# Sending a block's second half of output rows from the next block, and the last one behind all branches

## The chip, the cores and the metric

One core of one Trainium2 chip. The metric is the time of one execution on the device in microseconds (us), the median of several runs. Engine names are those of the profile: PE (TensorE matmul), DVE (VectorE), ACT (ScalarE), POOL (GpSimd), SP (SyncE); a q behind a name marks the engine's sequencer, which handles waits, branches and semaphore counts.

## The reference

Three stages on 4608 tokens of 512 numbers:

```python
attn = softmax(q @ mean8(k).T / 8); x = attn @ mean8(v)     # 8 batches, 8 heads
x = softplus(x @ w_in) @ w_out                              # 512 -> 2048 -> 512
do = x @ w_skip > 0                                         # tokens that compute
e = argmax(x @ w_gate); gate = softmax(x @ w_gate)[e]       # one of 8 experts
out = x;  out[do] = x + gate * (relu(x @ w1[e]) @ w2[e])    # 512 -> 1024 -> 512
```

The change lies in the last stage, the experts.

## The kernel before

The first two stages run over 9 groups of 512 tokens (up to 907 us of the span) and leave every token's row, with its gate weight, in a table in HBM; tokens that don't compute are written to `out` at once (L197). A table of token numbers, sorted by expert, says which rows belong together.

The expert stage (from 907 us) works on blocks of 256 rows of one expert: two halves of 128 rows. `superblock(i)` (L863) is one block. Blocks 0 to 9 are each in an If of their own (L870); from block 10 on the Ifs are nested (L964 to L967), each block inside that of the block before, so that the first block that doesn't exist skips all the rest with one jump. Twenty blocks run with these inputs. What a block does, by engine:

- PE multiplies the block's transposed rows with the first weight matrix (L898, 96 matmuls of 256 columns), then the result, half by half, with the second (L922 to L924, 24 matmuls of 512 columns for each half). The second half is in an If of its own in the nested blocks (L918), and is left out where a block has at most 128 rows: 38 halves are computed in 20 blocks.
- ACT and DVE take the results out of PSUM (L902, L903), split the next weights into two parts (`split1` L401, `split2` L409), and DVE makes the output rows of half j, `ys[j]` (L926).
- POOL issues the indirect DMAs, one after the other from one queue: the next block's weights (`fetch` L394), rows for later blocks (`gather` L354), token numbers for later blocks (`load_ids` L347), and the sends of `ys[0]` and `ys[1]` to `out` (L928), at the rows that `ids[i % 5]` names. Row numbers that don't exist are above the bounds and are dropped.

The order on each engine's queue is that of the code here (L932 switches the scheduler's reordering off). The framework adds the waits: the two sends write the same tensor, so the second waits until the first has landed; at an If whose body is skipped, each engine raises its own semaphore by what the body would have raised, and POOL does so for the semaphores of its DMAs, after it has waited for the DMAs that came before. At the end of the program SP waits for all semaphores, every engine drains, and POOL collects them all.

In a block, POOL's queue thus ends with

```python
nc.gpsimd.indirect_dma_start(
    out=out, out_offset=bass.IndirectOffsetOnAxis(ap=ids[i % 5][:, j:j + 1], axis=0),
    in_=ys[j], in_offset=None, bounds_check=NTOK - 1, oob_is_err=False)
```

for j = 0 and j = 1, and the next block begins with `fetch("raw1", w1, i + 1)` (L874).

Of the kernel before, what the change touches and what calls it, by code (L numbers as in the profile page):

```python
# [12 lines left out]
I32 = mybir.dt.int32  # L13
# [7 lines left out]
P = 128  # L21
# [9 lines left out]
BIG = float(1 << 20)  # L31
# [5 lines left out]
def tile_kernel(ctx, tc, qT, kT, vT, wbits, w9, w1, w2, out):  # L37
    nc = tc.nc
    NTOK = out.shape[0]
# [52 lines left out]
    ids = [const.tile([P, 2], I32, name=f"ids{i}") for i in range(5)]  # L92
# [251 lines left out]
    def at(i):  # L344
        return (lists[1], i) if i < NS1 else (lists[2], i - NS1)

    def load_ids(i):  # L347
        li, s = at(i)
        nc.gpsimd.indirect_dma_start(  # L349
            out=ids[i % 5], out_offset=None, in_=tab,  # L350
            in_offset=bass.IndirectOffsetOnAxis(ap=li["tidx"][:, s:s + 1], axis=0),
            bounds_check=P * NCOL // 2 - 1, oob_is_err=False)

    def gather(i):  # L354
        rows = NTOK - G if i < NS1 else NTOK
        for j in range(2):
            nc.gpsimd.indirect_dma_start(  # L357
                out=xg[i % 4][j], out_offset=None, in_=x2d[:rows, :],
                in_offset=bass.IndirectOffsetOnAxis(ap=ids[i % 5][:, j:j + 1], axis=0),
                bounds_check=rows - 1, oob_is_err=False)  # L360

    def flip(i, ps, tag):
        for half in range(2):
            tr = ps.tile([P, 512], F32, tag=tag, name="tr").rearrange("p (a b) -> p a b", a=2)
            for k2 in range(2):
                kk = half * 2 + k2
                for j in range(2):
                    nc.tensor.transpose(tr[:, k2, j * P:(j + 1) * P],
                                        xg[i % 4][j][:, kk * P:(kk + 1) * P], ident)
            h = xth[i % 2][:, half * 2:half * 2 + 2, :]  # L370
            nc.scalar.activation(out=h, in_=tr, func=AF.Copy)
            nc.vector.tensor_tensor(out=xtl[i % 2][:, half * 2:half * 2 + 2, :], in0=tr,
                                    in1=h.bitcast(F32), op=ALU.subtract)
# [3 lines left out]
    def spread(i):  # L377
        view = xd[0].rearrange("p (d k j r) -> p j k d r", d=4, k=4, j=2)
        for j in range(2):
            nc.vector.transpose(out=view[:, j], in_=xg[i % 4][j][:, :D].rearrange("p (k d r) -> p k d r", k=4, d=4))  # L380
        src = xd[0].rearrange("p (d x) -> p d x", d=4)
        dst = xm[i % 2].rearrange("p (q x) -> p q x", q=4)
        for q in range(4):
            for d in range(4):
                nc.sync.dma_start(out=dst[32 * d:32 * d + 32, q], in_=src[32 * q:32 * q + 32, d])

    def turn(i):
        xv = xm[i % 2].rearrange("p (q k j r) -> p j q k r", q=4, k=4, j=2)
        hv, lv = (t.rearrange("p k (j q r) -> p j q k r", j=2, q=4) for t in (xth[i % 2], xtl[i % 2]))
        for j in range(2):  # L390
            nc.scalar.activation(out=hv[:, j], in_=xv[:, j], func=AF.Copy)
            nc.vector.tensor_tensor(out=lv[:, j], in0=xv[:, j], in1=hv[:, j].bitcast(F32), op=ALU.subtract)

    def fetch(name, src, i):  # L394
        li, s = at(i)
        nc.gpsimd.indirect_dma_start(  # L396
            out=ws[name], out_offset=None, in_=src,
            in_offset=bass.IndirectOffsetOnAxis(ap=li["widx"][:, s:s + 1], axis=0),
            bounds_check=NE * P - 1, oob_is_err=False)
# [9 lines left out]
    def split2():  # L409
        raw = ws["raw2"].rearrange("p (a b) -> p a b", a=8)  # L410
        for q in range(4):
            cs = slice(q * 2, (q + 1) * 2)
            nc.scalar.activation(out=ws["w2h"][:, cs, :], in_=raw[:, cs, :], func=AF.Copy)  # L413
            nc.vector.tensor_tensor(out=ws["w2l"][:, cs, :], in0=raw[:, cs, :],  # L414
                                    in1=ws["w2h"][:, cs, :].bitcast(F32), op=ALU.subtract)
# [5 lines left out]
    with ExitStack() as ph:  # L421
# [4 lines left out]
        ap = ph.enter_context(tc.tile_pool(name="ap", bufs=2))  # L426
# [420 lines left out]
    ex = ctx.enter_context(tc.tile_pool(name="ex", bufs=1))  # L847
# [12 lines left out]
    xm[1] = ex.tile([P, 2 * D], F32, name="xm1")  # L860
    ys = [ex.tile([P, D], F32, name=f"ys{j}") for j in range(2)]

    def superblock(i, cond, mask, more, big=None):  # L863

        _, s = at(i)

        def changes(s_):
            return (mask & (1 << s_)) > 0

        with ExitStack() as st:  # L870
            if cond is not None:
                st.enter_context(tc.If(cond))
            if more > 0:
                fetch("raw1", w1, i + 1)  # L874
            if i == 0 and more > 0:
                gather(1)
                gather(2)
            if more > 2:
                gather(i + 3)
            if more > 3:  # L880
                load_ids(i + 4)
            if i > 0 and i != NS1 - 1:
                with tc.If(changes(s)):
                    split2()
            if more > 0:
                fetch("raw2", w2, i + 1)
            if more > 1 and i not in (0, NS1):
                spread(i + 2)
            xh, xl = xth[i % 2], xtl[i % 2]
            for fp in range(4):  # L890
                h = ps_f.tile([P, 2, SB], F32, tag="h", name="h")
                for f2 in range(2):
                    f0 = (fp * 2 + f2) * P
                    n = 0
                    for kk in range(4):
                        wh, wl = ws["w1h"][:, kk, f0:f0 + P], ws["w1l"][:, kk, f0:f0 + P]
                        for l, r in ((wh, xh), (wh, xl), (wl, xh)):
                            nc.tensor.matmul(h[:, f2, :], lhsT=l, rhs=r[:, kk, :],  # L898
                                             start=n == 0, stop=n == 11)
                            n += 1  # L900
                fs = slice(fp * 2, fp * 2 + 2)
                nc.scalar.activation(out=hh[:, fs, :], in_=h, func=AF.Relu)  # L902
                nc.vector.scalar_tensor_tensor(out=hl[:, fs, :], in0=h, scalar=0.0,  # L903
                                               in1=hh[:, fs, :].bitcast(F32),
                                               op0=ALU.max, op1=ALU.subtract)
                if fp == 1 and i > 0 and more > 0:
                    turn(i + 1)
            if more > 0:
                if i == 0:
                    flip(1, ps_t, "t")  # L910
                with tc.If(changes(s + 1)):
                    split1()
            if more > 1 and i in (0, NS1):
                spread(i + 2)
            for j in range(2):
                with ExitStack() as half:  # L916
                    if j and big is not None:
                        half.enter_context(tc.If((big & (32 << s)) > 0))  # L918
                    y = ps_o.tile([P, D], F32, tag=f"y{j}", name=f"y{j}")
                    js = slice(j * P, (j + 1) * P)  # L920
                    for f in range(8):
                        nc.tensor.matmul(y, lhsT=hh[:, f, js], rhs=ws["w2h"][:, f, :], start=f == 0, stop=False)  # L922
                        nc.tensor.matmul(y, lhsT=hh[:, f, js], rhs=ws["w2l"][:, f, :], start=False, stop=False)  # L923
                        nc.tensor.matmul(y, lhsT=hl[:, f, js], rhs=ws["w2h"][:, f, :], start=False, stop=f == 7)  # L924
                    r = xg[i % 4][j]
                    nc.vector.scalar_tensor_tensor(out=ys[j], in0=y, scalar=r[:, D:D + 1],  # L926
                                                   in1=r[:, :D], op0=ALU.mult, op1=ALU.add)
                nc.gpsimd.indirect_dma_start(  # L928
                    out=out, out_offset=bass.IndirectOffsetOnAxis(ap=ids[i % 5][:, j:j + 1], axis=0),
                    in_=ys[j], in_offset=None, bounds_check=NTOK - 1, oob_is_err=False)  # L930

    ctx.enter_context(tc.manual_schedule())  # L932
    o2 = order2()
# [30 lines left out]
    with ExitStack() as st:  # L964
        for i in range(NS2):
            st.enter_context(tc.If((n2 & 31) > i))
            superblock(NS1 + i, None, m2, NS2 - 1 - i, n2)  # L967


def _layout(q, k, v, moe_w_in, moe_w_out, moe2_w_skip, moe2_w_gate, moe2_w1, moe2_w2):  # L970
# [44 lines left out]
```

## Time and profile before

| | |
|---|---|
| median of 3 runs | 1376.26 us (1374.75 to 1378.42) |
| the profiled execution's own time | 1372.43 us |
| its span, first to last instruction | 1370.6 us |
| PE busy | 1336.9 us, 98% of the span |
| DVE busy | 847.9 us, 62% |
| ACT busy | 594.5 us, 43% |
| POOL busy | 309.5 us, 23% |

The span is 1.8 us shorter than the time of the same execution, and that time is 3.8 us under the median of the runs. Busy shares are averages over the whole program; a wait is read in the stage where it lies. In the rows further down, times are us from the span's start, and "idle before" is the engine's idle time ahead of the instruction with what ended it.

### The profile page before, as it was taken

The page shows a single profiled execution, that of the slowest core. Times are in us where ns is not written, and L with a number is a line of the kernel's source. Part 1 is how long each engine was busy: PE and PEld are TensorE (multiplying, and loading weights), DVE is VectorE, ACT ScalarE, POOL GpSimd, SP SyncE. Part 2 cuts the span into 40 slices and gives each one's busy share as a digit, 9 for nine tenths or more (in the row PEclk, how much of TensorE's full clock was granted, in tenths as well). Part 3 has the DMA queues.
Part 4 walks back from the last instruction along what each step waited for, and adds up shares of the span by engine and source line. Part 5 has one row for each costly group of instructions (what it writes and reads, how often), then busy time and mean ns, then how long its engine had stood idle before and what let it go on. Part 6 is the DMA issues. An engine that isn't in the chain of part 4 may idle for free. (4 is left out here: it accounts for less than half of the span.)

```text
span 1370.6 us, 21360 instructions
## 1 busy us (share of the span) xinstructions
PE 1336.9 (98%) x7030; PEld 1113.8 (81%) x7030; DVE 847.9 (62%) x1951; ACT 594.5 (43%) x1076; POOL 309.5 (23%) x374
## 2 busy tenths in 40 slices
PE   6999999999999999999999999999999999999986
PEld 5777887878878778778778878888989998889886
DVE  7997884974974965956947839534645432325254
ACT  6995554545445545545445445541111111114142
POOL 2010111121121030020120210342424243323332
PEclk9999999999999999999999999999999999999998
DMA  8643442241341340431411302513323122225272
GB/s 276 250 148 86 116 109 63 79 126 32 97 114 34 109 119 7 127 96 41 125 43 48 95 9 58 182 47 86 96 68 108 57 76 66 76 62 169 64 275 76
DMA packets 149600, 134.18 MB, mean 98 GB/s; under 512 B 100789, under 2 KB 116789, under 8 KB 146912
## 3 DMA queue, kind: packets, MB, share of 16 engines
q1 hardware_dynamic: 131744, 95.51, 24.1%
q0 software_dynamic: 17728, 37.13, 8.5%
q8 instruction: 60, 0.98, 0.3%
q14 instruction: 68, 0.56, 0.1%
HBM read 166.67 MB, written 29.67 MB: 143 GB/s over the span
## 5 line engine op out<-in xcount | busy, mean ns | idle before, releaser
L716 PE MATMUL h<-xh,wt 128*128 128x512 f32 x1152 | 379.6, 390 | 0.3 <-DVE xl L573 0.3
L716 PEld LDWEIGHTS h<-xh,wt 128*128 128x128 f32 x1152 | 216.2, 188 | 46.0 <-DVE xl L573 1.2
L898 PE MATMUL h<-xt,w1h 128*128 128x256 f32 x1280 | 229.2, 282 | 6.2 <-issue 2.8
L740 PE MATMUL y<-wt,gh 128*128 128x512 f32 x576 | 232.8, 404 | 0.0
L120 DVE CUSTOM_DVE_ANT_0 junk<-rows,w9b 128x512 bf16<-128x512 f32 x324 | 223.1, 689 | 8.1 <-ACT rows L114 3.2
L741 PE MATMUL y<-wt,gh 128*128 128x512 f32 x576 | 225.2, 391 | 0.0
L742 PE MATMUL y<-wt,gl 128*128 128x512 f32 x576 | 225.1, 391 | 0.0
L716 PE MATMUL h<-xl,wt 128*128 128x512 f32 x576 | 224.7, 390 | 0.0
L898 PEld LDWEIGHTS h<-xt,w1h 128*128 128x128 f32 x1280 | 197.9, 189 | 10.2 <-issue 5.6
L898 PE MATMUL h<-xt,w1l 128*128 128x256 f32 x640 | 180.3, 282 | 1.9 <-DVE w1l L406 0.8
L902 ACT ACTIVATE hs<-h 128x512 fp32r<-128x512 f32 x80 | 47.5, 597 | 310.5 <-PE h L898 159.2
L725 DVE SCALAR_TENSOR_TENSOR a<-h,a 128x512 f32<-128x512 f32 x144 | 98.8, 686 | 103.3 <-ACT a L724 102.5
L722 ACT ACTIVATE a<-h 128x512 f32<-128x512 f32 x144 | 85.8, 596 | 174.1 <-PE h L716 162.3
L727 ACT ACTIVATE gh<-a 128x512 fp32r<-128x512 f32 x144 | 91.0, 632 | 161.5 <-DVE a L725 159.7
L740 PEld LDWEIGHTS y<-wt,gh 128*128 128x128 f32 x576 | 108.2, 188 | 35.2 <-ACT a L722 7.3
L742 PEld LDWEIGHTS y<-wt,gl 128*128 128x128 f32 x576 | 108.1, 188 | 25.3 <-issue 2.1
L716 PEld LDWEIGHTS h<-xl,wt 128*128 128x128 f32 x576 | 108.2, 188 | 22.4 <-issue 0.2
L898 PEld LDWEIGHTS h<-xt,w1l 128*128 128x128 f32 x640 | 122.8, 192 | 2.5 <-DVE w1l L406 1.0
L741 PEld LDWEIGHTS y<-wt,gh 128*128 128x128 f32 x576 | 108.3, 188 | 20.0 <-issue 0.2
L729 DVE TENSOR_TENSOR gl<-a,gh 128x512 fp32r<-128x512 f32 x144 | 101.2, 702 | 37.4 <-ACT gh L727 34.0
L922 PE MATMUL y<-w2h,hs 128*128 128x512 f32 x304 | 119.1, 392 | 0.0
L924 PE MATMUL y<-w2h,hs 128*128 128x512 f32 x304 | 118.9, 391 | 0.0
(198 smaller groups left out, 1733.2 us busy)
## 6 DMA issues: line engine op xcount, KB each, us to landing
w9b<-w SPq DMA_DIRECT2D x81, 256.0 KB
raw<-wbits SPq DMA_DIRECT2D x12, 1024.0 KB
x2d<-rows SPq DMA_DIRECT2D x36, 260.0 KB
et<-q SPq DMA_DIRECT2D x256, 32.0 KB
kv<-vT SPq DMA_DIRECT2D x28, 288.0 KB
kv<-kT SPq DMA_DIRECT2D x24, 288.0 KB
xm<-misc SPq DMA_DIRECT2D x160, 32.0 KB
misc<-misc SPq DMA_DIRECT2D x144, 32.0 KB
```

The source lines that it names most:

```text
L120: nc.vector.tensor_tensor_reduce(out=ws["junk"], in0=rows[t][:, :D], in1=w9b[e], scale=1.0, scalar=0.0, op0=ALU.mult, op1=ALU.add, accum_o ...
L716: nc.tensor.matmul(h, lhsT=l, rhs=r[:, kk, :], start=n == 0, stop=n == 11)
L722: nc.scalar.activation(out=a, in_=h, func=AF.Abs)
L725: nc.vector.scalar_tensor_tensor(out=a, in0=h, scalar=0.0, in1=a, op0=ALU.max, op1=ALU.add)
L727: nc.scalar.activation(out=gh, in_=a, func=AF.Copy)
L729: nc.vector.tensor_tensor(out=gl, in0=a, in1=gh.bitcast(F32), op=ALU.subtract)
L740: nc.tensor.matmul(y, lhsT=th, rhs=wh, start=c == 0, stop=False)
L741: nc.tensor.matmul(y, lhsT=th, rhs=wl, start=False, stop=False)
L742: nc.tensor.matmul(y, lhsT=tl, rhs=wh, start=False, stop=c == 15)
L898: nc.tensor.matmul(h[:, f2, :], lhsT=l, rhs=r[:, kk, :], start=n == 0, stop=n == 11)
L922: nc.tensor.matmul(y, lhsT=hh[:, f, js], rhs=ws["w2h"][:, f, :], start=f == 0, stop=False)
L924: nc.tensor.matmul(y, lhsT=hl[:, f, js], rhs=ws["w2h"][:, f, :], start=False, stop=f == 7)
```

## The change

A column of row numbers, `idl`, is added. After the second half of a block DVE copies that block's second column of `ids` into it. POOL sends the first half as before; the second half is sent by the next block's first instruction, inside that block's If, from `idl` and `ys[1]`, and after the last If of the program there is one more such send.

```diff
--- before.py
+++ after.py
@@ -860,6 +860,14 @@
     xm[1] = ex.tile([P, 2 * D], F32, name="xm1")
     ys = [ex.tile([P, D], F32, name=f"ys{j}") for j in range(2)]
 
+    idl = ex.tile([P, 1], I32, name="idl")
+    nc.vector.memset(idl, int(BIG))
+
+    def send(where, rows):
+        nc.gpsimd.indirect_dma_start(
+            out=out, out_offset=bass.IndirectOffsetOnAxis(ap=where, axis=0),
+            in_=rows, in_offset=None, bounds_check=NTOK - 1, oob_is_err=False)
+
     def superblock(i, cond, mask, more, big=None):
 
         _, s = at(i)
@@ -870,6 +878,8 @@
         with ExitStack() as st:
             if cond is not None:
                 st.enter_context(tc.If(cond))
+            if i > 0:
+                send(idl, ys[1])
             if more > 0:
                 fetch("raw1", w1, i + 1)
             if i == 0 and more > 0:
@@ -925,9 +935,10 @@
                     r = xg[i % 4][j]
                     nc.vector.scalar_tensor_tensor(out=ys[j], in0=y, scalar=r[:, D:D + 1],
                                                    in1=r[:, :D], op0=ALU.mult, op1=ALU.add)
-                nc.gpsimd.indirect_dma_start(
-                    out=out, out_offset=bass.IndirectOffsetOnAxis(ap=ids[i % 5][:, j:j + 1], axis=0),
-                    in_=ys[j], in_offset=None, bounds_check=NTOK - 1, oob_is_err=False)
+                if j:
+                    nc.vector.tensor_copy(idl, ids[i % 5][:, 1:2])
+                else:
+                    send(ids[i % 5][:, 0:1], ys[0])
 
     ctx.enter_context(tc.manual_schedule())
     o2 = order2()
@@ -965,6 +976,7 @@
         for i in range(NS2):
             st.enter_context(tc.If((n2 & 31) > i))
             superblock(NS1 + i, None, m2, NS2 - 1 - i, n2)
+    send(idl, ys[1])
 
 
 def _layout(q, k, v, moe_w_in, moe_w_out, moe2_w_skip, moe2_w_gate, moe2_w1, moe2_w2):
```

How the rows move. First POOL's queue at the border of blocks 0 and 1 (`raw` is the first weight matrix of the coming block, `ys_8497` and `ys_8498` are the two halves' rows, ISA is the count for a skipped body). Before:

```order
L928 DMA out<-ys_8497,ids_123 4608x512
L928 DMA out<-ys_8498,ids_123 4608x512
L870 UNCONDITIONAL_BRANCH
L870 ISA
L870 UNCONDITIONAL_BRANCH
L870 COMPARE_AND_BRANCH
L396 DMA raw_8089<-w,misc 128x4096
```

and with the change:

```order
L867 DMA out<-ys_8497,ids_123 4608x512
L878 UNCONDITIONAL_BRANCH
L878 ISA
L878 UNCONDITIONAL_BRANCH
L878 COMPARE_AND_BRANCH
L867 DMA out<-ys_8498,idl 4608x512
L396 DMA raw_8089<-w,misc 128x4096
```

The second send has moved from one side of the branch to the other; it is still behind the first send and ahead of the weights. Next POOL's queue at the end of the program, with the semaphores that each row waits for (DVE_49 is the count of DVE's finished instructions, DMASW are those of POOL's DMAs). Before:

```order
L928 DMA out<-ys_8498,ids_124 4608x512 [waits DMASW2_49,DVE_49]
L964 UNCONDITIONAL_BRANCH
L964 ISA [waits DMASW3_49,DMASW2_49]
...
L964 ISA [waits DMASW4_49,DMASW5_49,DMASW3_49,DMASW6_49,DMASW2_49,DMASW7_49,DMASW1_49,DMASW0_49]
L964 UNCONDITIONAL_BRANCH
L1011 ISA [waits barrier_Pool_Activation_PE_DVE_SP_gather]
```

and with the change:

```order
L926 UNCONDITIONAL_BRANCH x2
L975 UNCONDITIONAL_BRANCH
L975 ISA [waits DMASW2_49,DMASW1_49]
...
L975 UNCONDITIONAL_BRANCH
L867 DMA out<-ys_8498,idl 4608x512 [waits DMASW4_49,DMASW3_49,DMASW5_49,DMASW2_49,DMASW6_49,DMASW1_49,DMASW7_49,DMASW0_49,DVE_49]
L1023 UNCONDITIONAL_BRANCH
L1023 ISA [waits barrier_Pool_Activation_PE_DVE_SP_gather]
```

The last send has moved behind the counts of the skipped blocks; the DVE count that it waits for is the one of the joined program, which DVE reaches only when it too has counted the skipped blocks (of the ISA rows one is executed, that of the first skipped block). Last, DVE's queue at the end of the last block that is written down. Before:

```order
L926 SCALAR_TENSOR_TENSOR ys_8498<-y_15453,xg_8492 128x512
L916 UNCONDITIONAL_BRANCH x2
L964 UNCONDITIONAL_BRANCH x18
```

and with the change:

```order
L936 SCALAR_TENSOR_TENSOR ys_8498<-y_15481,xg_8492 128x512
L926 UNCONDITIONAL_BRANCH x2
L939 COPY idl<-ids_124 128x1
L975 UNCONDITIONAL_BRANCH x18
```

The copy stands between the making of the rows and the branch that leads out of the block.

## Rows read from the trace of the kernel before

**Rows 1.** The expert part and the tail, by stretch: busy us (count) per engine

```profile
core 0: us, PE busy (x) PEld busy (x) DVE busy (x) ACT busy (x) POOL busy (x), PEclk, DMA share, GB/s
907.00:1139.00 232.00, 228.43 (x1471) 207.20 (x1470) 104.21 (x250) 36.70 (x65) 88.19 (x88) 0.99 0.29 81
1139.00:1360.00 221.00, 214.83 (x1390) 195.12 (x1389) 91.42 (x122) 56.86 (x84) 75.73 (x70) 0.99 0.37 119
1360.00:1371.00 11.00, 0.00 (x0) 0.00 (x0) 0.62 (x1) 0.00 (x0) 1.00 (x1) 0.68 0.07 21
```

**Rows 2.** Timeline of POOL, 1316.5 to 1336 us: start, us, instruction, [idle before <-releaser]

```profile
1321.18 1.36 POOL L928 DMA_INDIRECT out<-ys,ids  x1 [2.95 <-DVE w2l L414]
1322.85 2.01 POOL L396 DMA_INDIRECT raw<-w,misc  x1 [0.31 <-ACT hs L902]
```

**Rows 3.** Timeline of ACT, then PE, 1326 to 1338 us

```profile
1333.83 3.90 ACT L405 ACTIVATE w1h<-raw 128x1024 fp32r<-128x1024 f32 x4 [5.04 <-DMA raw<-w,misc]
...
1334.94 0.50 PE L898 MATMUL h<-xt,w1h 128*128 128x256 f32 x2 [1.53 <-ACT w1h L405]
```

**Rows 4.** Timeline of POOL, 1110 to 1140 us

```profile
1120.14 0.97 POOL L197 DMA_INDIRECT out<-rows,mi  x1 [2.54 <-ACT hs L902]
...
1131.36 1.00 POOL L396 DMA_INDIRECT raw<-w,misc  x1 [0.30 <-issue]
...
1138.92 1.01 POOL L928 DMA_INDIRECT out<-ys,ids  x1 [2.89 <-DVEq L960]
```

**Rows 5.** Timeline of DVE, 905 to 914 us

```profile
913.33 0.69 DVE L903 SCALAR_TENSOR_TENSOR hs<-h,hs 128x512 fp32r<-128x512 f32 x1 [4.32 <-issue]
```

**Rows 6.** One line, L231: count, duration ns min/median/max, first and last start

```profile
L231 DVE COPY misc<-misc x6: 150/166/170, 841.0 to 1053.5; 128x1 f32<-128x1 f32 x2, 128x2 f32<-128x2 f32 x2, 128x4 f32<-128x4 f32 x2
```

**Rows 7.** Timeline of DVE, then POOL, 1354 to 1362 us

```profile
1354.42 0.75 DVE L926 SCALAR_TENSOR_TENSOR ys<-y,xg 128x512 f32<-128x512 f32 x1 [2.38 <-PE y L924]
1359.87 0.75 DVE L926 SCALAR_TENSOR_TENSOR ys<-y,xg 128x512 f32<-128x512 f32 x1 [4.69 <-PE y L924]
...
1355.46 1.03 POOL L928 DMA_INDIRECT out<-ys,ids  x1 [3.04 <-DVE ys L926]
1361.10 1.00 POOL L928 DMA_INDIRECT out<-ys,ids  x1 [4.62 <-DVE ys L926]
```

**Rows 8.** The chain that ended last, in order of time: start, us, what

```profile
1340.49 2.40 DMA out<-ys,ids
...
1355.46 4.85 DMA out<-ys,ids
```

**Rows 9.** One line, L964, 1349 to 1371 us: branches and counts

```profile
L964 SPq EVENT_SEMAPHORE  x8: 17/17/17, 1360.9 to 1361.5; - x8
L964 POOLq EVENT_SEMAPHORE  x4: 17/43/43, 1364.0 to 1364.5; - x4
...
L964 SPq COMPARE_BRANCH  x2: 43/46/50, 1359.7 to 1361.6; - x2
L964 DVEq COMPARE_BRANCH  x2: 47/55/63, 1360.1 to 1363.7; - x2
L964 POOLq COMPARE_BRANCH  x2: 43/46/50, 1360.9 to 1365.7; - x2
...
L964 DVEq EVENT_SEMAPHORE  x1: 21/21/21, 1363.6 to 1363.6; - x1
L964 POOLq INC_SWDGE_SEM  x1: 1128/1128/1128, 1364.6 to 1364.6; - x1
```

**Rows 10.** One line, L1011, 1354 to 1371 us: the program's end

```profile
L1011 SPq EVENT_SEMAPHORE  x14: 17/28/28, 1365.6 to 1370.6; - x14
L1011 POOLq EVENT_SEMAPHORE  x4: 17/17/17, 1369.8 to 1370.5; - x4
L1011 POOLq DRAIN  x3: 51/103/3911, 1365.9 to 1370.3; - x3
L1011 SPq DRAIN  x3: 7/7/13, 1366.4 to 1370.0; - x3
```

## The prediction

> **What bounds the kernel now.** First the busy time by stretches. The last 464 us are the expert part [rows 1]. PE is busy 228.43 of 232.00 us in its first half and 214.83 of 221.00 us in its second, so PE is the bound, and all that could be won inside the blocks is its idle time, 3.57 + 6.17 = 9.7 us. In the same stretches DVE is busy 104.21 and 91.42 us, and POOL 88.19 and 75.73 us; both have room. The third row is the tail: from 1360.00 us on PE does nothing, and 11 us pass in which hardly anything is computed. The change lies at the borders of the blocks and in this tail, so I read the two places one after the other.
>
> At the border of two blocks POOL sends the second half (1321.18 us, after an idle time of 2.95 us) and then fetches the next first weight matrix (1322.85 us, 0.31 us after the send) [rows 2]. That fetch can matter: ACT waits 5.04 us for it before it splits the weights at 1333.83, and PE waits 1.53 us for ACT at 1334.94 [rows 3]. So whatever delays POOL's weight fetch here delays PE.
>
> In the tail the chain is this. DVE makes the last rows from 1359.87 to 1360.62, POOL issues their send at 1361.10 for 1.00 us [rows 7]. Meanwhile each engine jumps over the blocks that don't exist: SP's branch at 1359.7 is followed by its counts at 1360.9 (1.2 us later), DVE's at 1360.1 by 1363.6 (3.5 us), POOL's at 1360.9 by 1364.0 (3.1 us) [rows 9]. POOL's last count is at 1364.5, its count for the DMAs starts at 1364.6 and lasts 1.13 us; since it waits for the DMAs, the send of 1361.10 landed by 1364.5, at most 3.4 us after its issue. Then SP takes its waits from 1365.6 to its drain at 1366.4 (0.8 us), and POOL drains from 1365.9 for 3.91 us, to 1369.8; the engines' handshake takes the rest, to 1370.6 (0.8 us) [rows 10]. The last thing that anyone waits for before is thus POOL's drain, not the landing of the send.
>
> The sum below is made against the profiled execution: 1372.43 us, of which 1370.6 are span and 1.8 lie around it. It is 3.8 us under the median of 1376.26, and I carry the difference over to the median. A measurement of this kernel can tell about 0.3%, 4.1 us, from no change.
>
> **The change, part by part.** *At the borders.* POOL's order stays: first send, second send, weights. Only the branch has moved from behind the second send to ahead of it. The branch thus falls into the wait that the second send has anyway (2.95 us), and the 0.31 us between send and fetch may shrink [rows 2]. That is a gain of at most 0.3 us at a border where PE waits for the weights, and nothing elsewhere; a few such borders of the second stretch give 0 to -1.5 us, and I take 0, since PE's wait of 1.53 us had its cause mostly in the transfer and not in the branch [rows 3]. Two more sends are issued than before (the halves that don't exist are 2 of 40, and now their sends repeat older rows): 2 x 1.0 us of POOL [rows 7], covered by a POOL that is idle two thirds of the stretch.
>
> In the blocks that are not nested, other work that stood ahead of the branch stays ahead of the moved send: the writes of tokens that don't compute (1120.14), gathers, token numbers, and in block 8 also the fetch at 1131.36, before the send at 1138.92 [rows 4]. There the second send now starts some microseconds later or earlier against that work. Its rows, `ys[1]`, are written again only a block later (453 us for 20 blocks, so some 22 us), and a send lands 2.40 to 4.85 us after its issue [rows 8], so no one waits for it: 0. With that send later, the work that stood behind it can only come sooner.
>
> *The copies.* Each of 20 blocks gets a DVE copy of 128x1. The nearest rows are the small copies, 150 to 170 ns, two of them of this shape [rows 6]: 20 x 0.17 = 3.4 us. DVE is busy 42% of the stretch [rows 1], and its idle time at the end of a block is the cover (2.38 us before the first half's rows, 4.69 before the second's [rows 7]). Without that cover it would be +3.4 us. The copy also waits until the send that reads the old `idl` has landed; that was issued a block before. The memset before block 0 stands in DVE's idle time of 4.32 us ahead of 913.33 [rows 5]. All this I cost at 0.
>
> *The tail.* Here the last send has moved behind the branches, and it waits for a count that DVE gives only when it too has jumped. Step by step: rows made until 1360.62; the copy adds 0.17 to 0.24. DVE's branch was handled at 1360.1, while the rows were still being made [rows 7, 9]; with one more instruction ahead of it I take 1360.9 (0.8 later; between 0 and 0.8). The jump takes 3.5 us as before: 1364.4. From the end of DVE's work to POOL's send it takes 0.29 us (1354.42 + 0.75 to 1355.46 [rows 7]): the send starts at 1364.7, 3.6 us later than before. POOL's own jump and its count no longer stand in the way: its branch can come right behind the first send, at about 1356.5, the jump takes 3.1 us, that first send has landed by 1360.3 (1355.46 + 4.85 [rows 8]), and the count takes 1.13 us: 1361.4, some 3 us ahead of DVE.
>
> The send lands 3.4 us after 1364.7 (between 2.40 and 4.85 [rows 8]): 1368.1. No count for DMAs stands behind it, which saves the 1.13 us. SP's waits end 0.8 later, 1368.9. POOL's drain starts at 1365.9, 0.2 us behind the send's own end at 1365.7; what its 3.91 us are made of is not to be seen, and this is the unknown of the sum. I take the same length behind the same kind of work: 1365.9 + 3.9 = 1369.8, with the handshake 1370.6. That is the end of before: **0.0 us**. The lower end, a drain that is no longer than POOL's other two (0.05 and 0.10 us [rows 10]), leaves the landing as the last: 1368.9 + 0.8 = 1369.7, -0.9 us. The upper end is a drain that counts from the send: it ended 8.7 us after the send's issue (1361.10 to 1369.8), which gives 1373.4 and 1374.2 with the handshake, +3.6 us.
>
> The price of the landing can be weighed against a rule. The Trainium skill, "DMA: Bandwidth & Descriptors", section "Anatomy of one DMA — SWDGE (gpsimd) path", fits such a transfer as about 2.0 us plus its bytes at 436 GB/s, which makes an estimate of 2.6 us for these 256 KB where the rows say at most 3.4; by it the landing would come 0.8 us sooner, behind a drain that ends later anyway, and the sum would stay 0.0.
>
> Against the change speaks what the jumps show: 3.5 and 3.1 us on two engines, 1.2 on the third [rows 9], and one of the long ones now stands ahead of the last send, where before it lay beside it. The Trainium skill, "Runtime: NRT & Kernel Launch", section "Instruction fetch mechanics", says that a taken branch out of the fetched window has to fetch its target first; by that rule DVE pays its jump again, as in the sum. No row here shows the fetch itself.
>
> **The rivals.**
> *A: the long drain belonged to the count for the DMAs, not to the send.* For it: the count of 1.13 us is POOL's last work before the drain, 0.2 us ahead of it. Against it: the send too is work that may have to be drained. With that count some 4 us earlier, its 3.9 us are over before the landing: -0.9 us, 1375.4.
> *B, the slower side: the drain's end hangs on the last send.* It decides if the drain lasts until something that starts with the send's issue is done, beyond the landing that the counts show. For it: 3.91 us is long for an engine that has nothing left. Against it: the landing was already seen at 1364.5. It gives +3.6 us, 1379.9; with the slow landing of 4.85 in place of 3.4 it is +5.1, 1381.4.
> *C: the copies lie on PE's path.* +3.4 us, 1379.7. Against it speaks DVE's idle time at every place that I read.
> *D, clearly faster: a short jump and no drain.* If DVE jumps in SP's 1.2 us, because the target lies elsewhere in its changed queue, and the landing takes 2.40: 1360.9 + 1.2 + 0.3 + 2.4 + 0.8 + 0.8 = 1366.4, -4.2 us, 1372.1. It needs the low end of three costs at once.
> *That the change does nothing* is, at the borders, the forecast itself: the same three issues in the same order.
>
> **How the numbers follow.** Forecast (0.0: 1376.3) 0.43, A 0.20, B 0.20, C 0.05, D 0.12. A, the forecast and most of B and C lie within 4.1 us of 1376.26. Beyond it on the slow side I count 0.07 of B (the slow landing) and 0.01 of C; on the fast side D. So faster 0.12, within 0.3% 0.80, slower 0.08. The range goes from D's 1372.0 to B's and C's 1380.0 and leaves out B with the slow landing and what the median itself moves (1374.75 to 1378.42 in three runs).
>
> **What would show it.** In the profile after: the last send about 3.6 us later, near 1364.7, with DVE's count just ahead of it; no count for the DMAs behind it; POOL's drain about 3.9 us long, starting at about 1365.9 (short for A, past 1372 for B); PE's idle time in the two stretches still near 3.6 and 6.2 us (several us more for C). I am wrong if the time of the blocks moves by more than 2 us, above all if PE waits longer for the first weight matrix, or if the jumps change their length.

## The result, and the profile after

The changed kernel took 1390.9 us (median of 6 runs, 1388.14 to 1394.18) against 1376.22 us of the kernel before: ratio 1.0105, 95% interval 1.0087 to 1.0122. It is 14.7 us slower, where no difference was forecast and the range ended at 1380.0.

The same stretches of the expert part as in [rows 1], after; the last row is the tail.

```profile
core 0: us, PE busy (x) PEld busy (x) DVE busy (x) ACT busy (x) POOL busy (x), PEclk, DMA share, GB/s
907.00:1139.00 232.00, 220.03 (x1406) 197.48 (x1405) 101.89 (x256) 35.70 (x64) 87.09 (x86) 0.99 0.27 79
1139.00:1377.00 238.00, 226.72 (x1460) 205.01 (x1460) 95.35 (x136) 58.44 (x87) 76.69 (x71) 1.00 0.35 113
1377.00:1387.00 10.00, 0.13 (x1) 0.00 (x0) 0.81 (x2) 0.00 (x0) 1.00 (x1) 0.64 0.07 24
```

PE is idle for 12.0 and 11.3 us, where it was 3.6 and 6.2. So the loss is in the blocks, not in the tail. Cut by block (from the first matmul of one block's first product to that of the next), blocks 5 to 9 of the kernel before:

```profile
1026.09:1048.35 22.26, 22.26 (x148) 20.20 (x146) 9.12 (x26) 3.67 (x7) 8.19 (x11) 1.00 0.39 122
1048.35:1070.64 22.29, 22.29 (x148) 20.41 (x147) 11.75 (x41) 3.43 (x6) 8.22 (x8) 1.00 0.26 72
1070.64:1092.82 22.18, 22.18 (x145) 20.32 (x144) 9.99 (x30) 3.44 (x6) 8.04 (x8) 1.00 0.17 49
1092.82:1115.81 22.99, 22.99 (x154) 21.07 (x152) 7.98 (x19) 3.54 (x7) 11.11 (x11) 1.00 0.24 70
1115.81:1137.68 21.87, 21.87 (x147) 19.99 (x146) 6.16 (x10) 3.39 (x6) 9.05 (x9) 1.00 0.26 74
```

The same blocks after:

```profile
1026.31:1051.10 24.79, 22.87 (x148) 20.32 (x146) 9.09 (x27) 3.55 (x7) 7.66 (x11) 1.00 0.36 109
1051.10:1075.42 24.32, 22.89 (x147) 20.32 (x147) 11.57 (x42) 3.33 (x6) 9.57 (x10) 1.00 0.23 66
1075.42:1098.46 23.04, 22.36 (x145) 20.45 (x144) 9.91 (x31) 3.44 (x6) 7.28 (x8) 1.00 0.16 47
1098.46:1127.42 28.96, 26.02 (x154) 22.78 (x152) 8.10 (x20) 3.54 (x7) 11.87 (x12) 0.94 0.20 56
1127.42:1152.70 25.28, 22.90 (x147) 20.36 (x146) 6.12 (x11) 3.27 (x6) 8.06 (x8) 1.00 0.23 64
```

These five blocks take 126.4 us in place of 111.6: 14.8 us of the 16.0 by which the span grew. Block 8 alone loses 6.0. There the work in POOL's queue falls at another point of PE's work. Timeline of POOL, before, where the first product of block 8 runs from 1092.82 to 1104:

```profile
1097.61 0.97 POOL L197 DMA_INDIRECT out<-rows,mi  x1 [2.55 <-DMA out<-ys,ids]
1100.47 1.03 POOL L197 DMA_INDIRECT out<-rows,mi  x1 [1.88 <-ACT xt L391]
1101.81 1.05 POOL L357 DMA_INDIRECT xg<-x2d,ids  x1 [0.30 <-issue]
...
1109.70 1.00 POOL L396 DMA_INDIRECT raw<-w,misc  x1 [0.30 <-issue]
```

and after, where it begins at 1098.46:

```profile
1097.92 1.01 POOL L197 DMA_INDIRECT out<-rows,mi  x1 [2.57 <-DMA out<-ys,ids]
1100.76 0.97 POOL L197 DMA_INDIRECT out<-rows,mi  x1 [1.83 <-issue]
1102.03 1.05 POOL L357 DMA_INDIRECT xg<-x2d,ids  x1 [0.30 <-DVEq L893]
...
1108.91 1.03 POOL L867 DMA_INDIRECT out<-ys,idl  x1 [0.30 <-issue]
...
1111.57 0.99 POOL L396 DMA_INDIRECT raw<-w,misc  x1 [0.31 <-issue]
```

Before, the first token write (L197) waits until block 7's second send has landed. After, that send stands behind it, so it waits for the first send alone. Seen from the block's start, the gathers come 5.4 us sooner (3.6 against 9.0), and with the send between them eight transfers (1102.03 to 1112.56) follow one another without a pause in the first product. What PE does meanwhile is seen at ACT, which takes the four parts of the first product (`hs`) when PE's count for each is there. Timeline of ACT in block 8, before, then after (x2 is two parts):

```profile
1095.90 0.60 ACT L902 ACTIVATE hs<-h 128x512 fp32r<-128x512 f32 x1 [10.52 <-PE h L898]
1098.73 0.60 ACT L902 ACTIVATE hs<-h 128x512 fp32r<-128x512 f32 x1 [2.23 <-PE h L898]
1101.55 0.60 ACT L902 ACTIVATE hs<-h 128x512 fp32r<-128x512 f32 x1 [1.18 <-issue]
1104.38 0.60 ACT L902 ACTIVATE hs<-h 128x512 fp32r<-128x512 f32 x1 [2.23 <-PE h L898]
```

```profile
1101.54 0.60 ACT L912 ACTIVATE hs<-h 128x512 fp32r<-128x512 f32 x1 [13.11 <-DVE misc L338]
1105.21 0.60 ACT L912 ACTIVATE hs<-h 128x512 fp32r<-128x512 f32 x1 [3.07 <-PE h L908]
1113.96 1.34 ACT L912 ACTIVATE hs<-h 128x512 fp32r<-128x512 f32 x2 [7.11 <-issue]
```

Before, the parts come 3.1, 5.9, 8.7 and 11.6 us behind the block's start, a step of 2.8. After, they come at 3.1, 6.8 and 15.5: PE's counts are late ("late counts" from here on), and the third comes 1.4 us after POOL's last issue ends (1112.56). PE itself is held from 1108.4 on (timeline of PE, the first two such rows):

```profile
1109.48 0.37 PE L908 MATMUL h<-xt,w1l 128*128 128x256 f32 x1 [1.04 <-issue]
1110.20 0.28 PE L908 MATMUL h<-xt,w1h 128*128 128x256 f32 x1 [0.34 <-issue]
```

"issue" means that it waits for nothing that the profile shows. It doesn't look as if PE had run out of instructions: between 1102 and 1114.5 the trace has no packet of the two instruction queues, and the next one starts at 1114.97, when PE is already running again. Behind these gaps (PE busy 2.47 of 5.20 us from 1108.4 to 1113.6, granted clock 1.00) the granted clock fell to its lower level, 1.2 GHz (PEclk 0.51), for 3.4 us, in which a matmul of 512 columns started every 0.43 us in place of 0.23; as an estimate from that, 1.6 us of the block's 6.0:

```profile
1113.60:1117.00 3.40, 3.19 (x9) 2.66 (x9) 1.39 (x2) 1.20 (x2) 0.00 (x0) 0.51 0.02 5
```

The tail after, which answers to [rows 7, 9, 10]: timeline of DVE and of POOL, then the branches and counts (L975) and the program's end (L1023).

```profile
1377.17 0.75 DVE L936 SCALAR_TENSOR_TENSOR ys<-y,xg 128x512 f32<-128x512 f32 x1 [4.69 <-PE y L934]
1377.84 0.14 DVE L939 COPY idl<-ids 128x1 int32<-128x1 int32 x1
...
1380.73 1.00 POOL L867 DMA_INDIRECT out<-ys,idl  x1 [6.94 <-DVEq L975]
```

```profile
L975 DVEq COMPARE_BRANCH  x2: 47/55/63, 1377.6 to 1380.5; - x2
...
L975 POOLq INC_SWDGE_SEM  x1: 1128/1128/1128, 1377.1 to 1377.1; - x1
...
L975 DVEq EVENT_SEMAPHORE  x1: 21/21/21, 1380.4 to 1380.4; - x1
```

```profile
L1023 SPq EVENT_SEMAPHORE  x14: 17/28/2805, 1380.3 to 1386.5; - x14
L1023 POOLq EVENT_SEMAPHORE  x4: 17/17/17, 1385.8 to 1386.5; - x4
L1023 POOLq DRAIN  x3: 51/109/5237, 1380.5 to 1386.3; - x3
L1023 SPq DRAIN  x3: 7/7/13, 1383.9 to 1386.0; - x3
```

From the start of DVE's last rows to the end it is 9.4 us (1377.17 to 1386.6), before 10.7 (1359.87 to 1370.6). The tail became 1.3 us shorter.

### The profile page after: what moved, and what is told of

It is laid out like the page before. It is cut to its first block, busy times and chain, and to the rows that moved or that the text cites. A ratio compares the mean times of both kernels' runs of the same rounds, so it can differ in the third digit from the quotient of the medians.

```text
span 1386.6 us, 21369 instructions
## 1 busy us (share of the span) xinstructions
PE 1340.4 (97%) x7030; PEld 1113.9 (80%) x7030; DVE 848.1 (61%) x1972; ACT 593.7 (43%) x1076; POOL 309.5 (22%) x374
## 5 line engine op out<-in xcount | busy, mean ns | idle before, releaser
L742 PEld LDWEIGHTS y<-wt,gl 128*128 128x128 f32 x576 | 108.1, 188 | 25.4 <-issue 2.1
```

The source lines that it names most:

```text
L742: nc.tensor.matmul(y, lhsT=tl, rhs=wh, start=False, stop=c == 15)
```

## The experiments

Each set was run together with the kernel before on one chip, and each on another chip. The kernel before took 1371.9, 1370.6, 1362.5, 1362.3 and 1375.8 us in the five sets; each ratio stands against the runs of its own set. Block lengths are worked out from the starts of the first products; blocks 12 to 14 stand for the nested ones. The two rows without a set are the traces of the result; every row is one profiled execution. "The bookkeeping" is what POOL issues between two blocks that are not nested: token writes (L197), table writes and gathers.

```
set kernel          5     6     7     8     9   12 to 14
    before        22.3  22.3  22.2  23.0  21.9  22.9 to 23.0
    after         24.8  24.3  23.0  29.0  25.3  23.0 to 23.3
1   only5to9      22.5  22.6  22.6  29.2  24.5  22.5 to 23.2
1   allbut5to9    22.3  22.3  22.2  23.0  21.9  22.8 to 22.9
1   outsideif     22.3  22.3  22.2  23.0  22.3  22.9 to 23.2
2   behind        24.2  23.0  22.9  29.1  24.2  22.2
2   twice         23.2  22.8  23.5  23.0  22.3  23.2 to 23.4
2   rowsearly     22.3  22.3  22.2  24.6  24.3  22.7 to 23.4
2   twomoved      26.2  22.7  22.5  23.0  21.9  22.9 to 23.3
3   emptynine     22.3  22.3  22.2  25.5  22.3  22.2
4   after2        22.3  22.3  22.2  23.0  21.9  22.2
4   before2       22.3  22.3  22.2  23.0  21.9  22.2
5   emptynine3    22.3  22.4  22.2  31.9  21.9  23.0 to 23.3
5   twoplaces2    22.3  22.3  22.2  23.0  21.9  22.2
```

Two blocks that the table leaves out scatter as well where counts are late, also in kernels that leave them as they were: block 0 takes 24.9 to 27.6 us in place of 22.8, block 11 up to 26.4 in place of 22.2.

### First set: which borders lose

**only5to9**: of the change, the sends by blocks 5 to 9 alone.

```diff
-            if i > 0:
+            if i > 0 and 4 <= i - 1 <= 8:
...
-                if j:
+                if j and 4 <= i <= 8:
...
-                    send(ids[i % 5][:, 0:1], ys[0])
+                    send(ids[i % 5][:, j:j + 1], ys[j])
...
-    send(idl, ys[1])
```

> Only the second halves of blocks 4 to 8 are deferred (sent by blocks 5 to 9, where token writes and table writes stand ahead of the send in POOL's queue); all others are sent in their own block and nothing is sent behind the branches. Theory Q (queue): the send has moved behind POOL's waits for the bookkeeping, so that weights, rows and token numbers of blocks 5 to 9 are issued some 1.3 us later, and PE loses its time there: between the two traces the blocks from 5 to 9 take 14.8 us more. It expects +13 to +16 us against the kernel before. Theory S (spread: the copy, the wait for it and the jump cost something at every border): +3 to +4 us, a quarter of the loss.

Measured: 1381.12 against 1371.9 us, ratio 1.0069 (1.0052 to 1.0085), +9.2 us. Less than theory Q's sum, over twice theory S's. Blocks 8 and 9 lose as in the change; blocks 5 to 7 lose only 0.9 us, in the change 5.4 with the same order of POOL's queue there.

**allbut5to9**: the other borders, with `not 4 <= ... <= 8` in the two conditions and the last send kept.

> All second halves are deferred as in the change, but those of blocks 4 to 8, which are sent in their own block. Theory Q: the loss is gone, -2 to +2 us against the kernel before (in the traces the tail became 1.3 us shorter, block 11 took 1.5 us more). Theory S: three quarters of the loss stay, +10 to +12 us.

Measured: 1369.41, ratio 0.9992 (0.9981 to 1.0003). The loss is gone: it lies at the five borders that theory Q names. By what it comes about there is the question of the second set.

**lastalone**: `i - 1 == 19` and `i == 19` in the two conditions.

> Only the last block's second half is deferred, behind all branches; every other send stands in its own block. It prices the tail by itself: the prediction had 0.0 us with a drain that stays long, -0.9 with a short one, +3.6 with one that counts from the send; the two traces show a tail that is 1.3 us shorter. Theory Q and theory S both expect -1.5 to 0 us; +3 us or more would mean that the deferred last send does cost and was hidden in the comparison of the traces.

Measured: 1370.7, ratio 0.9992 (0.9982 to 1.0001), -1.2 us, as expected from the tail.

**outsideif**: behind the If, ahead of the bookkeeping.

```diff
-            if i > 0:
+            if i > NS1:
                 send(idl, ys[1])
...
         superblock(i, n1 > i, m1, NS1 - 1 - i)
+        send(idl, ys[1])
```

> In the first ten blocks the second half is deferred past the branch alone: the send stands right behind the If, ahead of the bookkeeping's table and token writes, weights and rows; from block 10 on all is as in the change. Theory Q: what counts is the bookkeeping that the send was moved behind, not the branch, so the loss is gone: -2 to +2 us. A theory B (branch: the send has to wait for the join and the DVE copy, and this alone delays what follows) expects the full loss, +12 us or more. Theory S: +10 to +14 us.

Measured: 1370.01, ratio 0.9986 (0.9976 to 0.9996). Past the branch the send costs nothing; behind the bookkeeping it does.

### Second set: late weights, or rows that come sooner

**behind**: the two lines `if i > 0: send(idl, ys[1])` moved behind `fetch("raw2", w2, i + 1)`.

> As the change, but in every block the deferred send stands behind the next weights, the rows and the token numbers in POOL's queue (right behind the second weight matrix). Theory L (late): weights and rows of blocks 5 to 9 come late because a send of 1.0 us stands ahead of them; then the loss is gone here, -2 to +1 us against the kernel before. Theory G (gathers): blocks 8 and 9 lose because the token writes no longer wait for the second send's landing, so that the rows are gathered sooner and land while PE is in the first product of the block (in the change they are issued 3.6 to 7.5 us behind its start, before at 9.0 to 13.0); this stays, so block 8 takes about 29 us again in place of 23 and block 9 about 25 in place of 22, and only blocks 5 to 7 are cured: +6 to +10 us.

Measured: 1372.94 against 1370.62, ratio 1.0017 (1.0007 to 1.0027). The sum fits neither theory, the blocks do: 29.1 and 24.2 us in blocks 8 and 9 as theory G has it, though weights and rows have no send ahead of them, which speaks against theory L (and the late weights of theory Q). Blocks 5 to 7, which G expected to be cured, still lose 3.3 us. What hides it in the sum is that most nested blocks take 22.2 us here.

**twice**: in-block sends as before, and a second one at the start of blocks 5 to 9.

```diff
-            if i > 0:
+            if 5 <= i <= 9:
                 send(idl, ys[1])
...
+                send(ids[i % 5][:, j:j + 1], ys[j])
                 if j:
                     nc.vector.tensor_copy(idl, ids[i % 5][:, 1:2])
-                else:
-                    send(ids[i % 5][:, 0:1], ys[0])
...
-    send(idl, ys[1])
```

> Every second half is sent in its own block as in the kernel before, and those of blocks 4 to 8 once more by blocks 5 to 9, where the change sends them (the same rows to the same places); each block also has the copy. Theory L: the second send is as much in the way of weights and rows as in the change: +9 to +14 us. Theory G: the token writes of blocks 8 and 9 wait for the in-block send as before, so the rows come late there and these two blocks keep their 23 and 22 us; blocks 5 to 7 may lose part of their 5.3 us: 0 to +5 us.

Measured: 1376.88, ratio 1.0049 (1.0032 to 1.0066), +6.3 us, between the two. Blocks 8 and 9 are nearly whole, as theory G has it; blocks 5 to 7 lose 2.7 us. Blocks 2 to 4 stay at 22.2 us with the copy in each, so the copies are covered.

**rowsearly**: in the kernel before, block 7's gathers moved.

```diff
         superblock(i, n1 > i, m1, NS1 - 1 - i)
+        if i == NS1 - 3:
+            gather(NS1)
+            gather(NS1 + 1)
+            load_ids(NS1 + 2)
...
-        elif i == NS1 - 3:
-            gather(NS1)
-            gather(NS1 + 1)
-            load_ids(NS1 + 2)
```

> The kernel before with one edit: behind block 7 the four gathers and the token numbers stand ahead of the bookkeeping's steps in POOL's queue, so that they are issued some 6 us sooner and land while PE is in block 8's first product; no send is moved. Theory G: block 8 takes about 28 to 30 us in place of 23.0, +4 to +7 us. Theory L: rows that come sooner cost nothing, -1 to +1 us.

Measured: 1374.01, ratio 1.0028 (1.0014 to 1.0042), +3.4 us. Rows that come sooner do cost, with no send moved; but block 8 takes 24.6 us (and block 9, of which the expectation says nothing, 24.3 in place of 21.9), not 28 to 30. Landing rows are not the whole of it.

**twomoved**: only blocks 7 and 8 send behind their If.

```diff
-            if i > 0:
+            if i > 0 and i not in (8, 9):
                 send(idl, ys[1])
...
         superblock(i, n1 > i, m1, NS1 - 1 - i)
+        if i in (7, 8):
+            send(idl, ys[1])
```

> As the change, but the second halves of blocks 7 and 8 are sent right behind their If, ahead of the bookkeeping's token writes; the other 18 borders are as in the change. Theory G: blocks 8 and 9 are back at 23 and 22 us, and only the loss of blocks 5 to 7 stays: +3 to +7 us against the kernel before. If instead the whole row of deferred sends counts, it stays at +11 us or more.

Measured: 1375.44, ratio 1.0037 (1.0023 to 1.0052), +4.8 us. Blocks 8 and 9 are back at 23.0 and 21.9.

### Third to fifth set: what holds PE

In about two thirds of the blocks with late counts in the traces so far, a held count came 1.0 to 1.8 us behind the end of a row of POOL issues that had no pause (in blocks 2 to 4 it was 0.4 to 0.9), also in block 7 of the kernel before, where no rows are gathered. So the issues themselves came under suspicion. **emptynine** and **emptyfour** add transfers to the kernel before that move nothing, **busypool** memsets:

```diff
+    none = ex.tile([P, 1], I32, name="none")
+    nc.vector.memset(none, int(BIG))
+    scr = ex.tile([P, 2 * 9], I32, name="scr")
...
         superblock(i, n1 > i, m1, NS1 - 1 - i)
+        if i == 7:
+            for k in range(9):
+                nc.gpsimd.indirect_dma_start(
+                    out=scr[:, 2 * k:2 * k + 2], out_offset=None, in_=tab,
+                    in_offset=bass.IndirectOffsetOnAxis(ap=none, axis=0),
+                    bounds_check=P * NCOL // 2 - 1, oob_is_err=False)
```

(4 in place of 9; for busypool twelve `nc.gpsimd.memset(scr, 0.0)` of 128x512.)

> The kernel before with nine more indirect transfers on POOL behind block 7, ahead of the bookkeeping; all their row numbers are out of bounds, so they are issued at 1.0 us each and move no row. Theory P (issues in a row): what holds PE's counts in the first product is POOL issuing indirect transfers one after the other without a pause; over all runs the held counts come 1.2 to 1.5 us behind the last issue of such a row. Then block 8 takes 26 to 29 us in place of 23.0 although nothing lands. Theory G (the landing rows do it): block 8 keeps 23.0 us. Under both block 9 may take 2 to 3 us more, since the real gathers are pushed into it; in all +5 to +9 us (P) or 0 to +4 us (G).

> The same with four transfers that move no row. Theory P: the row ends early in the first product, PE's second count comes about 2 us late (8 us behind the start of the block in place of 5.9) and is caught up before PE runs dry: block 8 within 1.5 us of 23.0, in all 0 to +4 us with what is pushed into block 9. Theory G: the counts of block 8 come at 3.1, 5.9, 8.7 and 11.6 us as before.

> The kernel before with twelve memsets of 128x512 on POOL in the same place, so that POOL is busy without issuing transfers. Theory P: POOL's work alone does not hold PE's counts; in block 8 they come at 3.1, 5.9, 8.7 and 11.6 us as before while the memsets run. If any busy POOL held them, they would come late as in emptyfour or emptynine.

Measured: ratios 1.0024 (1.0013 to 1.0034), 1.0001 (0.9991 to 1.0010) and 1.0004 (0.9995 to 1.0014). But in this set PE's counts were on time in every kernel and nearly every block, whatever POOL issued. So the three tell nothing of what holds them. Block 8 of emptynine took 25.5 us because the real rows came late.

That raised the question whether the loss itself is there in such a set:

> The changed kernel again. If the loss is made by PE's late counts: on a chip where the kernel before shows counts at 3.1, 5.9, 8.7 and 11.6 us in blocks 5 to 9 (as all kernels of the last call), the change costs 0 to +4 us; where the counts come late, +12 to +16 us again. If the loss has another cause in the order of the transfers, it is +12 to +16 us on either chip.

> The kernel before again, for its trace on the same chip as after2: the time is that of the runs beside it (ratio 1.000). It shows whether the first product's counts are late here (blocks 11 to 14 take about 23 us) or not (22.2 us).

> Nine indirect transfers that move no row, ahead of the bookkeeping of block 8, again. If the counts are late on this chip: theory P (issues in a row) expects counts of block 8 at 12 us and later and its first product longer by 2 us or more; theory G (landing rows) expects them at 3.1, 5.9, 8.7, 11.6 us. If no kernel shows late counts here: block 8 about 25.5 us as in emptynine, through rows that come late.

> Block 7's gathers ahead of the bookkeeping, again. If the counts are late on this chip: block 8 about 24.6 and block 9 about 24.3 us, +3.4 us in all, as in rowsearly. If no kernel shows late counts here: 0 us, blocks 8 and 9 at 23.0 and 21.9.

Measured: after2 1360.71 against 1362.3 us, ratio **0.9986** (0.9976 to 0.9995); before2 1.0000 (0.9991 to 1.0010); emptynine2 1.0028 (1.0018 to 1.0037); rowsearly2 0.9998 (0.9988 to 1.0007). The same program that lost 14.7 us is 1.6 us faster here. Block 8 of after2 by ACT's timeline (it begins at 1087.4), with the same eight issues of POOL in a row:

```profile
1090.52 0.60 ACT L912 ACTIVATE hs<-h 128x512 fp32r<-128x512 f32 x1 [13.11 <-DVE misc L338]
1093.35 0.60 ACT L912 ACTIVATE hs<-h 128x512 fp32r<-128x512 f32 x1 [2.23 <-PE h L908]
1096.17 0.60 ACT L912 ACTIVATE hs<-h 128x512 fp32r<-128x512 f32 x1 [1.18 <-issue]
1099.00 0.60 ACT L912 ACTIVATE hs<-h 128x512 fp32r<-128x512 f32 x1 [2.23 <-PE h L908]
```

The last set met late counts again (the kernel before at 1375.81 us), and so could tell issues from rows:

> Nine indirect transfers that move no row, ahead of the bookkeeping of block 8, a third time. If blocks 11 to 14 take about 23 us here (late counts): theory P (issues in a row) expects block 8's later counts at 12 us and more and its first product longer by 2 us or more; theory G (landing rows) expects 3.1, 5.9, 8.7, 11.6 us in block 8. If they take 22.2 us: as emptynine and emptynine2, and P and G stay open.

Measured: 1384.99, ratio 1.0063 (1.0046 to 1.0080). Block 8 (from 1092.3) took 31.9 us, in emptynine2 25.4. POOL's first and last empty transfer, then ACT's timeline, then the stretch of the nine issues and the whole block:

```profile
1094.85 1.04 POOL L950 DMA_INDIRECT scr<-tab,none  x1 [0.30 <-issue]
...
1105.41 0.99 POOL L950 DMA_INDIRECT scr<-tab,none  x1 [0.31 <-issue]
```

```profile
1095.38 0.60 ACT L905 ACTIVATE hs<-h 128x512 fp32r<-128x512 f32 x1 [10.49 <-PE h L901]
1102.31 0.60 ACT L905 ACTIVATE hs<-h 128x512 fp32r<-128x512 f32 x1 [6.33 <-PE h L901]
1110.34 0.60 ACT L905 ACTIVATE hs<-h 128x512 fp32r<-128x512 f32 x1 [6.39 <-issue]
1115.54 0.60 ACT L905 ACTIVATE hs<-h 128x512 fp32r<-128x512 f32 x1 [4.61 <-remote]
```

```profile
1094.60:1106.60 12.00, 8.30 (x66) 7.97 (x66) 3.30 (x9) 2.23 (x4) 9.11 (x9) 1.00 0.07 22
1092.30:1124.20 31.90, 26.97 (x153) 23.70 (x152) 7.97 (x19) 3.52 (x7) 20.21 (x20) 0.89 0.17 46
```

The parts come at 3.1, 10.0, 18.0 and 23.2 us, and PE is busy for 8.3 of the 12 us, while 22 GB/s move: 64 packets are the 256 KB of block 7's send, the other 272 are under 512 bytes each, and no row is gathered. Issues without rows do it: theory P. (The real gathers are issued from 1110.94 on, so the fourth part falls among them; and of the 8.9 us that block 8 takes longer, about 2.4 may come from late rows, as in emptynine2.)

**twoplaces** joins outsideif for the first ten blocks and behind for the nested ones.

```diff
-            if i > 0:
-                send(idl, ys[1])
...
             if more > 0:
                 fetch("raw2", w2, i + 1)
+            if i > NS1:
+                send(idl, ys[1])
...
         superblock(i, n1 > i, m1, NS1 - 1 - i)
+        send(idl, ys[1])
```

> A version made of two of the runs: in the first ten blocks the deferred send stands right behind the If, ahead of the bookkeeping (as in outsideif), and from block 10 on behind the next weights, rows and token numbers (as in behind, where the blocks from 11 on took 22.2 us in place of about 23); the last one stands behind all branches. Adding the two: the tail about -1.5 us, blocks 11 to 19 about -8 us. Expected -7 to -11 us against the kernel before.

> The version of two places again. Without late counts (blocks 11 to 14 at 22.2 us in the kernel before): -5 us as in twoplaces, from the tail and block 19. With late counts: -7 to -11 us, since blocks 11 to 19 keep 22.2 us here.

Measured: ratio 0.9965 (0.9952 to 0.9979), -4.9 us, in the set with counts on time, and 0.9907 (0.9889 to 0.9926), -13.3 us, with late counts (expected -7 to -11; what the further 2 us are is not shown). It is faster than the kernel before in both sets; the change was not run beside it. In the nested blocks the weights and one gather are issued ahead of the first product, and the row of issues inside it is shorter (four in a row up to 6.2 us behind the start of block 12, in the kernel before six up to 8.8).

## Why the prediction was wrong

**The step that failed** is in the part on the borders: "no one waits for it: 0. With that send later, the work that stood behind it can only come sooner." The order was seen rightly, with block 8 named, and work that comes sooner was priced at nothing. It is what cost most, 9.4 of the 14.8 us: the gathers of blocks 8 and 9 moved from the second product into the first, and the token writes' wait for the second send, which had made a pause between POOL's issues, was gone (behind, rowsearly, twomoved). Blocks 5 to 7 lost the smaller part, 5.4 us. That the send's own issue, which had lain in the time in which POOL waits for the bookkeeping, now lengthened the row of issues behind it fits twice (2.7 us), but is argued and not shown: these three blocks lose 0.9 us in only5to9 and 4.7 in twomoved with the same order, one execution each. The prediction's own sign of being wrong, blocks that move by more than 2 us, came; but not by a longer wait for the first weight matrix, which it had in mind.

**Cover was counted as a share.** That the two more sends are "covered by a POOL that is idle two thirds of the stretch" took POOL's issues as a matter of POOL alone. In the sets with late counts they are a matter of PE: it can be held when POOL issues indirect transfers one after the other through its first product (emptynine3). No rival had this mechanism; C, the only one in the blocks, was about the copies, which cost nothing (twice). The sign that could have been seen stands in the trace of before: PE's idle time of 9.7 us in the expert part was taken as the most that could be won, without a question for its cause.

**The tail went as forecast in kind.** The send waited for DVE's jump (1380.43, send at 1380.73). POOL's own count was over 2.2 us ahead of it (1377.1 + 1.13). The drain ended at 1385.73 (1380.49 + 5.24), 4.0 us behind the send's end at 1381.73; before it had ended 4.1 us behind the count's end. In both traces it goes by POOL's last work: A (the drain belongs to the count) and B (8.7 us from the send; here 5.0) both fell. Three terms were mis-sized. The 0.8 us for one more instruction ahead of DVE's branch was 0.1 (the branch, at 1377.6, still lies inside the making of the rows: 0.4 us behind its start, before 0.3). The jump took 2.9 us, not 3.5. The landing took at most 2.6, not 3.4 (SP's wait of 2.805 us ended at 1383.4). The send came 3.6 us behind the start of DVE's rows, not 4.8, and the end 1.3 us sooner, not 0.0.

Of the two rules cited, the one on taken branches (the Trainium skill, "Runtime: NRT & Kernel Launch", section "Instruction fetch mechanics") agrees with the jump of 2.9 us that DVE paid again; no run shows the fetch. The fit of the Trainium skill, "DMA: Bandwidth & Descriptors", section "Anatomy of one DMA — SWDGE (gpsimd) path", gave an estimate of 2.6 us for the landing; the row after has the same 2.6 as its bound.

**Where PE's counts are on time, the forecast held**: after2 is 0.9986 of the kernel before, inside the 0.3% that was given 0.80, and its gain lies in the tail (9.5 us, in before2 10.3) and in block 18. But late counts are seen in the trace on which the prediction rests, as nested blocks of 23 us in place of 22.2, and the prediction did not ask about them.

**Open.** Why a set of runs has late counts is not known: the program is the same, and the kernel before takes 1370 to 1376 us with them and 1362 without. Each set had its own chip and its own time, so the two can't be told apart. Nor is a row of issues enough by itself where counts are late: in block 15 of the kernel before (from 1252.94) POOL issues six transfers from 1254.17 to 1263.90 without a pause, the first two of 2.0 us each, and the parts come at 3.1, 5.9, 8.8 and 12.0 us; the block takes 22.2 us in every trace. In block 8 of the kernel before such a row runs from 7.6 to 17.9 us, and the last two parts are on time. What sets these rows apart was not tried, nor whether landing rows add to the hold. Nor is it shown by what path POOL's issues hold PE's counts. The Trainium skill, "NOTIFIC — the notification-queue block", section "The write path", says that the path which writes trace records can hold the engine that makes them, when a queue or its own pipeline is full. No run here shows it. PE's instructions are most of those recorded (14060 of 21360 in the kernel before, weight loads included), and every run here lists a span and a clock from such records, so none tells whether the hold is there without them. That busy work on POOL without issues does nothing was seen only where counts were on time (busypool).

## What to carry to other kernels

When a transfer is moved past others in a queue, write down for each of them where it now falls against the bounding engine's work, also when it comes sooner: a wait that goes away may have been what kept a burst out of a sensitive stretch. If the bounding engine stands idle for no reason that the profile names, look what another queue issues just then, before calling that time the most that can be won. And repeat a result of one per cent in another set before building on its cause.

## What the hardware showed unexpectedly

- In some sets, indirect transfers issued by POOL one after the other hold PE's counts in a product of 256-column matmuls though no row is gathered (emptynine3: the second part at 10.0 us in place of 5.9, the third at 18.0 in place of 8.7). In other sets the same issues do nothing (emptynine2: 5.9 and 8.7), and some rows of issues cost a block nothing in any set (block 15).
- PE's records go on while its counts are already late: in block 5 of the kernel before ACT takes the third part at 1037.44, 11.4 us behind the start in place of 8.7, and PE's busy time is still 22.26 of 22.26 us. The last matmul of that part is recorded as ended at 1034.73; PE's count for it stands in the trace at 1037.36. Gaps appear where the counts are later than that. The line of ACT's timeline:

```profile
1037.44 0.60 ACT L902 ACTIVATE hs<-h 128x512 fp32r<-128x512 f32 x1 [3.80 <-remote]
```

- POOL's drain at the program's end is over some 4.0 us behind POOL's last work on transfers (4.1 us behind its count before, 4.0 behind the send's issue after). In both the last send had landed by then: 5.3 us earlier before, 2.4 us earlier after.
